# Windowed attention and ELU feed-forward on one core: the first chunk's probabilities kept in fp32 and turned on TensorE, and d_ff of the first two chunks in other parts

## The chip, the cores and the metric

The kernel runs on one core of a Trainium2 chip. The metric is the device time of one execution in microseconds. Before the change the median of three runs is 653.16 us (652.48 to 653.65).

## The reference

Causal attention with a window of 128 keys and 4 sink keys over 4 batches, 8 heads, 768 positions and a head size of 64, then a feed-forward over the 3072 tokens with 512 model columns, 2048 inner columns (d_ff) and ELU. The weights come in 64-bit floats, the rest in fp32.

```python
keep = is_sink | ((rel >= 0) & (rel < window))        # rel = query - key
scores = np.where(keep, q @ k.T / np.sqrt(D), -1e9)
a = np.exp(scores - scores.max(-1)); a = a / (a.sum(-1) + 1e-9)
x = (a @ v) laid out as [tokens, 512]
h = x @ w_in
out = np.where(h > 0, h, np.exp(np.minimum(h, 0)) - 1) @ w_out
```

## The kernel before

**Tiles.** Tokens are taken in 24 query tiles of 128, grouped into nine chunks (`SIZES`, L42: three of two tiles, six of three). Heads are taken in four pairs. A visit is one query tile of one head pair: its keys are its own tile and the one before it (the first tile of a batch has only its own), 132 columns each, the first 4 of them sinks.

**A visit (L572 to L683).** TensorE makes the scores of the two heads (L598 in the first chunks, fp32, one head on the upper and one on the lower 64 rows); VectorE adds the mask and takes the extremum (L617); ScalarE takes exp and the sum (L619); ScalarE or GpSimd scales the sum (L623) and VectorE inverts it (L624). Then the probabilities, times 1/sum, are split into two fp16 parts, high on ScalarE (L631) and low on VectorE (L632), into one tile `pq`. A DMA transpose from SyncE's queue (L650) turns `pq` into `pt`. V comes as a raw fp32 tile (`vs`, two buffers) and is split into fp16 high and low parts too (L545, L546). The values (L664) are three fp16 products for each head and key tile: high x high, low x high, high x low; later query tiles of a batch have sink values (L669) besides. The tiles of a chunk add up in one bank `po` for a head pair, from which x is taken in two fp16 parts (L701, L702).

**The feed-forward (L712 to L779).** For each of the 16 blocks f of d_ff: twelve products h of x and w_in (L729), ELU (exp on ScalarE, L737; L739 on VectorE or GpSimd; L740 on VectorE), split of g in two fp16 parts (L742, L743), and six products acc for a chunk of two tiles (nine for three) with w_out (L750). The weights stand in memory as 64-bit floats. Each half block is loaded (L434), rebuilt as fp32 by one ScalarE and three VectorE instructions (L305 to L308, through bank `acc[2]`), and split in fp16 parts by ScalarE (L455) and GpSimd (L456); its load waits for the high part of the half five before it. All halves then stay in SBUF.

**Order.** `PARTS` (L45) is the order of the feed-forward. Chunks 0 and 1 take turns over parts of d_ff. The sums of an unfinished part are stored to the output (L773) and added back later (L770, L771). Everything is a task with an engine, a duration and what it depends on; a planner (`Plan`, L99) places the tasks by a list schedule, TensorE's by positions in slots (two for each block and chunk), the others by due times from the round before, and `keep_order` holds each engine to that order. `RINGS` (L54) says how many buffers a tile has; a writer waits for the users of the buffer's last turn. Where a task has two possible engines, the planner chooses.

```python
PARTS = [(0, 0, HALF), (1, 0, HALF), (0, HALF, NF), (1, HALF, NF)] + ...   # HALF = 10, NF = 16
tr = add("SP", 1.4, lambda ...: nc.sync.dma_start_transpose(pt[:, :nblk, :], ...), deps=parts + ...)
val = add("PE", ..., values, deps=[tr, ...], pos=at[k - j + nt - 1] + V_AT0 + 0.01 * j, line=2)
```

Of the kernel before, what the change touches and what calls it, by code (L numbers as in the profile page):

```python
# [9 lines left out]
F32 = mybir.dt.float32  # L10
# [5 lines left out]
AF = mybir.ActivationFunctionType  # L16
ALU = mybir.AluOpType
# [3 lines left out]
P = 128  # L21
B, H, S, D = 4, 8, 768, 64
# [4 lines left out]
NF = FF // P  # L27
NW = 2 * NF
NS = 4
KW = NS + P  # L30
MASKED = -1.0e31

P_SCALE, V_SCALE = 16384.0, 2048.0
X_SCALE, W_SCALE = 32.0, 256.0
PO_SCALE = X_SCALE / (P_SCALE * V_SCALE)
# [5 lines left out]

SIZES = (2, 2, 2, 3, 3, 3, 3, 3, 3)  # L42

HALF = 10
PARTS = [(0, 0, HALF), (1, 0, HALF), (0, HALF, NF), (1, HALF, NF)] + [(c, 0, NF) for c in range(2, len(SIZES))]  # L45
LAG = 2
ROUNDS = 8
VISIT = 3
WHOLE = 4
DUP = 4  # L50
AHEAD = 5
V_AT = 7
V_AT0 = 5.0
RINGS = dict(kqs=2, kq=3, vs=2, vm=1, vt=6, sk=2, e=3, st=6, pq=3, pt=6, g=2, gh=3, x=7, wv=4, s=2, po=1, h=2, wu=2, sv=2, wps=1, raw=6)  # L54


def key_tiles(ch):
# [15 lines left out]
VT = NP * P  # L73
# [25 lines left out]
class Plan:  # L99
# [7 lines left out]
    def add(self, eng, dur, fn, *args, deps=(), lat=0.0, pos=None, or_=None, line=0, slow=1.0, lock=True):  # L107

        t = Task(eng, dur, fn, args, deps, lat, pos, slow)
        t.line = line  # L110
        t.lock = lock
        if or_:
            t.ways[or_[0]] = or_[1:]
        self.tasks.append(t)
        return t

    def ring(self, name, writers, users):

# [172 lines left out]
def dma_us(nbytes):  # L291
    return nbytes / 330e3
# [69 lines left out]
def fast_path(tc, ctx, first, kq, vx, wt, out, nw, flag):  # L362

    nc = tc.nc
    wide = wt.dtype != F32
    pool = ctx.enter_context(tc.tile_pool(name="sb", bufs=1))
    psum = ctx.enter_context(tc.tile_pool(name="ps", bufs=1, space=PSUM))

    def rows(name, shape, dtype, n=None, mem=pool):
        return [mem.tile(shape, dtype, name=f"{name}{i}") for i in range(n or RINGS[name])]  # L370

# [29 lines left out]
    tmp = pts[-1].rearrange("p b k -> p (b k)").bitcast(F32)  # L401
    rest = make_masks(nc, tmp[:, : 4 * P], tmp[:, 4 * P : 4 * P + NS], nw, m0, m1, m2)
    nc.gpsimd.memset(ones, 1.0)
    for t in pqs:
        nc.gpsimd.memset(t[:, 8, :], 0.0)

    plan = Plan()
    add, ring = plan.add, plan.ring
    turn = {}

    def slot(name):
        turn[name] = turn.get(name, -1) + 1
        return turn[name] % RINGS[name]

    rest_ = add("DVE", 0.9, rest)
# [11 lines left out]
    first_acc2 = []  # L427

    def weights(k):
# [10 lines left out]

        ld = add("SP", 0.4, load, deps=[w_done.get(k - AHEAD, [None])[0]], lat=1.45)
        if wide:
# [21 lines left out]
    base, pos = {}, 0  # L464
    for c, f0, f1 in PARTS:
        base.setdefault(c, pos)
        pos += 2 * (f1 - f0)


    xs = {}  # L470
    x_at, x_old = [0, 0], []

# [15 lines left out]
        x_old.append((lo, hi, users))  # L488

    later = []  # L490
    v_of, sk_of = {}, {}

    def attention(c):
        ts = CHUNKS[c]
        nt, kts = len(ts), key_tiles(ts)
        nk = len(kts)
        kc, qc = nk * KW, nt * P
        n = NP * nt
        if c == 0:
            at = [-3.0 - V_AT0 - 3.0 + 1.2 * (k - n) for k in range(n)]  # L500
        elif c == 1:
            at = [-1.0 + k * (base[c] - 1.0 - V_AT) / (n - 1) for k in range(n)]
        else:
            at = [base[c] - 2.0 - V_AT - (n - 1 - k) * (base[c] - base[c - 1]) / n for k in range(n)]

        def split_keys(h):
# [27 lines left out]
            lo = buf[:, KQ_MAX : KQ_MAX + kc] if c >= DUP else buf[:, kw : 2 * kw]  # L534
            return hi, lo, th, tl, users

        def vtile(g):

            if g not in v_of:
                st, i = vs[slot("vs")], slot("vt")  # L540
                ld = None
                if g not in first["vs_"]:
                    ld = add("SP", 0.4, lambda: nc.sync.dma_start(st, vx[:, g * VT : (g + 1) * VT]), lat=dma_us(P * VT * 4))
                hi, lo, users = vh[i], vl[i], []
                va = add("ACT", act_us(VT), lambda: nc.scalar.activation(hi, st, AF.Copy, scale=V_SCALE), deps=[ld])  # L545
                vb = add("DVE", 0.13 + 0.00108 * VT, lambda: nc.vector.scalar_tensor_tensor(lo, st, V_SCALE, hi, ALU.mult, ALU.subtract), deps=[va], slow=1.5)  # L546
                ring("vs", [ld or va], [va, vb])
                ring("vt", [va], users)
                v_of[g] = hi, lo, va, vb, users
            return v_of[g]  # L550
# [14 lines left out]
        k = 0  # L565
        for p in range(NP):
# [3 lines left out]
            po = po_ps[slot("po")]  # L570
            vals, visit = [], []
            for g in ts:  # L572
                t, j = g % NT, ts.index(g)
                nb = 1 if t == 0 else 2
# [5 lines left out]
                e3 = es[slot("e")]  # L580
                sm = sts[slot("st")]
                mn, rs, tmp = sm[:, 0:2], sm[:, 2:4], sm[:, 4 : 4 + 2 * NS].rearrange("p (e k) -> p e k", e=2)
                pq = pqs[slot("pq")]
                pt = pts[slot("pt")]
# [29 lines left out]
                exps, st_users = [], []  # L614
# [7 lines left out]

                rr = add("ACT", 0.22, lambda rs=rs: nc.scalar.activation(rs, rs, AF.Copy, scale=1.0 / P_SCALE, bias=1.0e-9 / P_SCALE), deps=[ex for _, ex in exps], or_=("POOL", 0.2, lambda rs=rs: nc.gpsimd.tensor_scalar(rs, rs, 1.0e-9, 1.0 / P_SCALE, ALU.add, ALU.mult)))  # L623
                rr = add("DVE", 0.17, lambda rs=rs: nc.vector.reciprocal(rs, rs), deps=[rr])  # L624
                parts, his = [], []
                for e in range(2):
                    src = e3[:, e, :wd].rearrange("p (b k) -> p b k", k=KW)[:, :, NS:]
# [4 lines left out]
                    b = add("DVE", 0.478 if nb == 2 else 0.33, lambda src=src, hi=hi, lo=lo, re=re: nc.vector.scalar_tensor_tensor(lo, src, re, hi, ALU.mult, ALU.subtract), deps=[a], slow=1.5)  # L632
                    parts += [a, b]
                    his.append(a)
                if t >= 2:
# [8 lines left out]
                    b = add("POOL", 0.65, sinks, deps=[rr], lock=False)  # L644
# [27 lines left out]
                if nt < VISIT:  # L672
                    val = add("PE", dur + 0.19 + (0.2 if j == 0 else 0.0), values, deps=[tr, *(d for v in vts for d in v[2:4]), *(sk[1:2] if sk else [])], pos=at[k - j + nt - 1] + (V_AT0 if c == 0 else V_AT) + 0.01 * j, line=2)
                    ring("pt", [tr], [val])
# [5 lines left out]
                else:  # L680
                    users = []
# [3 lines left out]
            if visit:  # L685
# [4 lines left out]

                val = add("PE", sum(v[1] for v in visit) + 0.19, together, deps=[*(v[2] for v in visit), *(d for v in visit for u in v[4] for d in u[2:4]), *(v[5][1] for v in visit if v[5])], pos=at[k - 1] + V_AT, line=2)
                for v in visit:
# [5 lines left out]
                vals.append(val)  # L698

            xh, xl = x_room(qc)  # L700
            fa = add("ACT", act_us(qc, True), lambda xh=xh, po=po: nc.scalar.activation(xh, po[:, :qc], AF.Copy, scale=PO_SCALE), deps=[vals[-1]])  # L701
            fb = add("DVE", dve_us(qc) + 0.1, lambda xh=xh, xl=xl, po=po: nc.vector.scalar_tensor_tensor(xl, po[:, :qc], PO_SCALE, xh, ALU.mult, ALU.subtract), deps=[fa])  # L702
            ring("po", [vals[0]], [fa, fb])
            users = []
            x_taken(fa, users)
            xs[c, p] = xh, xl, fa, fb, users


    evacs = [None] * max(SIZES)
    evacs[2] = first_acc2[-1] if first_acc2 else None  # L710

    def feed_forward(c, f0, f1, start):  # L712
        nt = len(CHUNKS[c])
# [68 lines left out]
    start = 0  # L782
    for c, f0, f1 in PARTS:
        if f0 == 0:
# [32 lines left out]
    b = add("PE", 0.1, lambda: nc.tensor.matmul(sp[:, 0:3], ones, some16, start=True, stop=True), deps=[a], pos=start + 2 * LAG - 1.5)  # L817
# [251 lines left out]
```

## Time and profile before

| | us |
|---|---|
| median of three runs | 653.16 |
| the profiled execution, as timed | 653.45 |
| its span, first to last instruction | 651.7 |
| TensorE busy in it | 615.2 |
| VectorE busy | 429.7 |
| ScalarE busy | 427.4 |
| GpSimd busy | 355.6 |

Durations come from the one profiled execution. PE is TensorE's matmuls, PEld its weight loads, DVE VectorE, ACT ScalarE, POOL GpSimd, SP SyncE; a q behind a name is the engine's sequencer. L598 is line 598 of the kernel. An fp32 product shows as two instructions, and "x4" counts instructions. In a timeline the number behind the start runs from the first one's start to the last one's end.

### The profile page before, as it was taken

Reading aid. Unit: us, or ns where it says so; the run is one execution under the profiler, and the core shown is the slowest. Engines: PE = TensorE matmul, PEld = TensorE weight load, DVE = VectorE, ACT = ScalarE, POOL = GpSimd, SP = SyncE. Lnnn points to the kernel's source line nnn. Section 1 sums busy time; section 2 is a strip of 40 time slices with the busy share of each in tenths; the row PEclk is TensorE's granted clock in tenths of the full one; section 3 lists DMA queues with packets and bytes.
Section 4 is the critical chain, followed back from the end, with each engine's and each line's share of the span. In section 5 each row is a group of like instructions: output and inputs, shape, how many; then the busy total and the mean of one; then the engine's idle time right before and its main releaser. Section 6 shows DMA issues by size and latency. Waiting matters only on the chain.

```text
span 651.7 us, 13258 instructions
## 1 busy us (share of the span) xinstructions
PE 615.2 (94%) x4449; PEld 364.5 (56%) x4449; DVE 429.7 (66%) x1175; ACT 427.4 (66%) x1227; POOL 355.6 (55%) x622
## 2 busy tenths in 40 slices
PE   3598789999999999999999999999999999999995
PEld 1354456666667556565555656565555656555552
DVE  6899988877756775557577766668577766433222
ACT  4797868767767876667667776667666775432221
POOL 1187879673436776655556766555456665313221
PEclk9997889999999999999999999999999999999998
DMA  7898887376637565346444755456655734201001
GB/s 281 166 258 264 278 186 227 122 193 139 162 90 147 141 158 123 78 110 187 120 100 108 225 113 135 85 114 167 131 101 103 202 83 101 65 34 39 1 0 54
DMA packets 124348, 87.84 MB, mean 135 GB/s; under 512 B 104176, under 2 KB 104176, under 8 KB 124272
## 3 DMA queue, kind: packets, MB, share of 16 engines
q1 hardware_dynamic: 124272, 86.92, 53.1%
q8 instruction: 37, 0.61, 0.4%
q14 instruction: 39, 0.32, 0.2%
HBM read 54.39 MB, written 7.34 MB: 95 GB/s over the span
## 4 chain that ended last, share of the span: by engine, by line
PE 86%; DVE 6%; DMA 3%; ACT 2%; issue 2%; POOL 1%; SPq 0%; DVEq 0%; ACTq 0%
PE h L729 38%; PE acc L750 37%; PE po L664 5%; PE s L598 2%; PE s L591 2%; PE s L592 2%; DMA pt<-pq 1%; DVE wu L307 1%; DVE wv L308 1%; DVE pq L632 1%; ACT e L619 1%; DVE wu L306 1%; DMA vs<-in_vx_dram 1%; DMA words<-in_window_dram 1%; DVE e L617 1%
## 5 line engine op out<-in xcount | busy, mean ns | idle before, releaser
L729 PE MATMUL h<-x,w 128*128 128x384 f16 (+1 forms) x1728 | 279.2, 312 | 2.2 <-ACT x L701 1.4
L729 PEld LDWEIGHTS <-w 128*128 128x128 f16 x1728 | 166.0, 99 | 99.5 <-issue 2.8
L743 POOL TENSOR_TENSOR gl<-g,gh 128x384 f16<-128x384 f32 (+1 forms) x144 | 126.4, 878 | 138.9 <-ACT gh L742 105.3
L750 PE MATMUL acc<-w,gh 128*128 128x512 f16 x768 | 194.1, 382 | 0.0
L737 ACT ACTIVATE g<-h 128x384 f32<-128x384 f32 (+1 forms) x144 | 65.5, 455 | 108.8 <-PE h L729 96.2
L632 DVE SCALAR_TENSOR_TENSOR pq<-e,st,pq 128x256 f16<-128x256 f32 (+1 forms) x192 | 110.0, 605 | 15.2 <-ACT pq L631 14.9
L750 PEld LDWEIGHTS <-gh 128*128 128x128 f16 x768 | 71.4, 98 | 71.5 <-ACT g L737 1.7
L750 PE MATMUL acc<-w,gl 128*128 128x512 f16 x384 | 109.6, 380 | 0.4 <-POOL gl L743 0.3
L739 DVE TENSOR_SCALAR g<-g 128x384 f32<-128x384 f32 (+1 forms) x76 | 36.9, 485 | 102.0 <-ACT g L737 101.9
L619 ACT ACTIVATE e<-e,st 128x264 f32<-128x264 f32 (+1 forms) x192 | 93.2, 486 | 15.3 <-DVE st L617 13.9
L617 DVE CUSTOM_DVE_ANT_0 e<-s,m 128x264 f32<-128x264 f32 (+1 forms) x192 | 71.5, 405 | 47.5 <-PE s L592 36.1
L631 ACT ACTIVATE pq<-e,st 128x256 f16<-128x256 f32 (+1 forms) x192 | 85.0, 480 | 14.6 <-DVE st L624 7.7
L742 ACT ACTIVATE gh<-g 128x384 f16<-128x384 f32 (+1 forms) x144 | 69.5, 483 | 35.1 <-DVE g L740 33.2
L740 DVE SCALAR_TENSOR_TENSOR g<-g,h 128x384 f32<-128x384 f32 (+1 forms) x144 | 72.7, 505 | 17.9 <-POOL g L739 16.3
L750 PEld LDWEIGHTS <-gl 128*128 128x128 f16 x384 | 37.6, 98 | 46.9 <-POOL gl L743 1.4
L526 POOL TENSOR_TENSOR kq<-kqs,kq 128x528 fp32r<-128x528 f32 (+1 forms) x40 | 49.3, 1232 | 22.6 <-ACT kq L522 22.4
L456 POOL TENSOR_TENSOR w<-wv,w 128x256 f16<-128x256 f32 x64 | 46.9, 752 | 13.4 <-ACT w L455 13.0
L598 PE MATMUL s<-kqs 64*128 64x264 f32 (+1 forms) x144 | 33.8, 498 | 19.3 <-DVE st L617 11.7
L739 POOL TENSOR_SCALAR g<-g 128x384 f32<-128x384 f32 (+1 forms) x68 | 33.8, 498 | 32.5 <-ACT g L737 30.1
L664 PE MATMUL po<-pt,vh 128*64 128x128 f16 x704 | 41.5, 228 | 7.1 <-DMA pt<-pq 5.5
L522 ACT ACTIVATE kq<-kqs 128x912 fp32r<-128x912 f32 (+1 forms) x40 | 36.3, 913 | 14.3 <-PE s L592 11.8
L528 POOL TENSOR_TENSOR kq<-kqs,kq 64x384 fp32r<-64x384 f32 x40 | 41.1, 1026 | 3.1
(81 smaller groups left out, 638.2 us busy)
## 6 DMA issues: line engine op xcount, KB each, us to landing
raw<-in_wt_dram SPq DMA_DIRECT2D x32, 512.0 KB, 5.2
kqs<-in_kq_dram SPq DMA_DIRECT2D x24, 456.0 KB, 3.7
kqs<-in_kq_dram SPq DMA_DIRECT2D x20, 390.0 KB, 3.6
vs<-in_vx_dram SPq DMA_DIRECT2D x28, 256.0 KB, 3.5
out_dram<-wv SPq DMA_DIRECT2D x24, 256.0 KB, 3.1
vm<-in_vx_dram SPq DMA_DIRECT2D x6, 768.0 KB, 4.8
kqs<-in_kq_dram SPq DMA_DIRECT2D x8, 326.0 KB, 4.0
pt<-pq SPq DMA_TRANSPOSE x96, 3.2
```

The lines of the kernel that those rows point to most:

```text
L617: red = add("DVE", 0.24 + 0.001 * wd, lambda ee=ee, me=me, sp=sps[e], m=m, wd=wd: nc.vector.tensor_tensor_reduce(ee, sp[:, :wd], m[:, :wd] ...
L619: ex = add("ACT", 0.47 + 0.00085 * wd, lambda ee=ee, me=me, rs=rs[:, e : e + 1]: nc.scalar.activation(ee, ee, AF.Exp, bias=me, scale=-1.0, ...
L631: a = add("ACT", act_us(nb * P, True), lambda src=src, hi=hi, re=re: nc.scalar.activation(hi, src, AF.Copy, scale=re), deps=[rr])
L632: b = add("DVE", 0.478 if nb == 2 else 0.33, lambda src=src, hi=hi, lo=lo, re=re: nc.vector.scalar_tensor_tensor(lo, src, re, hi, ALU.mult ...
L664: nc.tensor.matmul(po[e * D : (e + 1) * D, oc], vts[i][x][:, vo : vo + D], pt[:, (2 * e + part) * nb + i, :], start=new, stop=last)
L729: nc.tensor.matmul(hp[:, :n], win[:, part, d, :], xx[:, :n], start=k == 0, stop=k == 3 * ND - 1)
L737: a = add("ACT", act_us(n) + 0.18, lambda gf=gf, hp=hp, sums=sums: nc.scalar.activation(gf, hp[:, :n], AF.Exp, scale=1.0 / G_SCALE, accum_ ...
L739: b = add("DVE", 0.14 + 0.00057 * n, lambda gf=gf: nc.vector.tensor_scalar(gf, gf, -1.0, G_SCALE, ALU.add, ALU.mult), deps=[a], slow=2.1, ...
L740: b = add("DVE", dve_us(n), lambda gf=gf, hp=hp: nc.vector.scalar_tensor_tensor(gf, gf, 0.0, hp[:, :n], ALU.min, ALU.max), deps=[b])
L742: th = add("ACT", act_us(n), lambda gf=gf, gh=gh: nc.scalar.activation(gh[:, :n], gf, AF.Copy), deps=[b])
L743: tl = add("POOL", pool_us(n), lambda gl=gl, gf=gf, gh=gh: nc.gpsimd.tensor_tensor(gl[:, :n], gf, gh[:, :n], ALU.subtract), deps=[th])
L750: nc.tensor.matmul(acc[i], gg[:, i * P : (i + 1) * P], wout[:, part, :], start=f == f0 and k == 0, stop=f == f1 - 1 and k == 2)
```

## The change

For chunk 0 (`c < PLAIN`, with `PLAIN = 1`) the probabilities are not split and not transposed by DMA. GpSimd multiplies an identity by 1/sum into a diagonal matrix for each head; TensorE multiplies the exponentials as the stationary operand with it, which turns and scales them at once, in fp32, into `acc[0]` or `acc[1]`; ScalarE or VectorE copies the result to the `pt` buffer; and the values are one fp32 product for each head and key tile, with the raw V tile. V tile 0 is no longer split at all, and the raw tiles 0 and 1 stay in their buffers until chunk 0's last values. The parts of d_ff become 7 blocks of chunk 0, 13 of chunk 1, 9 of chunk 0 and 3 of chunk 1, in place of 10, 10, 6 and 6.

```diff
-HALF = 10
-PARTS = [(0, 0, HALF), (1, 0, HALF), (0, HALF, NF), (1, HALF, NF)] + [(c, 0, NF) for c in range(2, len(SIZES))]
+HALF = NF // 2
+PARTS = [(0,0,7),(1,0,13),(0,7,16),(1,13,16)] + [(c, 0, NF) for c in range(2, len(SIZES))]
+PLAIN = 1
+T_AT = 3.5
+PE_T, PE_V = 0.25, 0.25
+    ident = pool.tile([P, P], F32, name="ident")
+    make_identity(nc, ident)
...
+        def vraw(g):
+            if g not in raw_of:
+                st, users = vs[slot("vs")], []
...
+                ring("vs", [ld] if ld else [], users)
+                raw_of[g] = st, ld, users
+            return raw_of[g]
...
+                if c < PLAIN:
...
+                    def diagonal(dg=dg, rs=rs):
+                        nc.gpsimd.tensor_tensor(dg, ident.unsqueeze(1).to_broadcast([P, 2, P]), rs.unsqueeze(2).to_broadcast([P, 2, P]), ALU.mult)
+                    def turned(tp=tp, dg=dg, e3=e3, nb=nb):
+                        for e in range(2):
+                            for i in range(nb):
+                                o = (e * nb + i) * P
+                                nc.tensor.matmul(tp[:, o : o + P], e3[:, e, i * KW + NS : (i + 1) * KW], dg[:, e, :], start=True, stop=True)
+                    dgs = add("POOL", pool_us(2 * P), diagonal, deps=[rr])
+                    tr = add("PE", PE_T * 2 * nb, turned, deps=[dgs], pos=at[k] + T_AT, line=3)
+                    ev = add("ACT", act_us(2 * nb * P), ..., deps=[tr, rest_], or_=("DVE", dve_us(2 * nb * P), ...))
...
+                    def values(po=po, vts=vts, ptf=ptf, j=j, nb=nb, p=p):
...
+                                nc.tensor.matmul(po[e * D : (e + 1) * D, oc], vts[i][0][:, vo : vo + D], ptf[:, (e * nb + i) * P : (e * nb + i + 1) * P], start=j == 0 and i == 0, stop=j == nt - 1 and i == nb - 1)
+                    val = add("PE", PE_V * 2 * nb, values, deps=[ev, *(v[1] for v in vts)], pos=at[k - j + nt - 1] + V_AT0 + 0.01 * j, line=2)
```

## Rows read from the trace of the kernel before

**Rows 1.** The page: busy us, share of the span and instructions of each engine

```profile
PE 615.2 (94%) x4449; PEld 364.5 (56%) x4449; DVE 429.7 (66%) x1175; ACT 427.4 (66%) x1227; POOL 355.6 (55%) x622
```

**Rows 2.** Stretches: length, busy us (count) by engine, granted clock, DMA share, GB/s

```profile
0.00:37.38 37.38, 18.72 (x117) 11.40 (x118) 28.27 (x113) 25.61 (x74) 9.68 (x34) 1.00 0.79 217
37.38:90.80 53.42, 42.98 (x313) 25.23 (x314) 49.91 (x124) 42.99 (x122) 44.29 (x82) 0.90 0.93 269
90.80:159.00 68.20, 68.20 (x536) 43.63 (x536) 53.26 (x136) 51.39 (x157) 47.56 (x90) 0.97 0.62 168
```

**Rows 3.** TensorE's waits over the span: us in total, times, longest

```profile
PE s L598 <- DVE st L617: 11.7, 10, 2.8
...
PE po L664 <- DMA pt<-pq: 5.5, 5, 1.9
```

**Rows 4.** The chain that ended last, in order: start us, us, what

```profile
27.68 0.85 PE po L664 x12
...
37.38 2.61 PE h L729 x12
...
46.66 4.57 DMA vs<-in_vx_dram
...
90.80 2.50 PE h L729 x12
...
95.19 1.31 PE h L729 x12
96.50 1.29 PE acc L750 x6
...
105.61 0.46 PE po L664 x12
...
111.83 0.65 PE s L598 x4
```

**Rows 5.** VectorE, 37.38 to 90.8 us, by shape: count, busy us, mean ns

```profile
L306 DVE TENSOR_SCALAR wu<-raw 128x512 uint16<-128x512 uint16 x15 | 10.3, 683 | 0.0
L308 DVE SCALAR_TENSOR_TENSOR wv<-acc,wu 128x512 int32<-128x512 int32 x15 | 10.2, 680 | 0.4 <-ACT acc L305 0.3
L307 DVE TENSOR_SCALAR wu<-raw 128x512 uint16<-128x512 uint16 x15 | 10.1, 674 | 0.0
L632 DVE SCALAR_TENSOR_TENSOR pq<-e,st,pq 128x256 f16<-128x256 f32 x16 | 8.3, 553 | 0.0
L617 DVE CUSTOM_DVE_ANT_0 e<-s,m 128x264 f32<-128x264 f32 x17 | 6.6, 418 | 0.0
L740 DVE SCALAR_TENSOR_TENSOR g<-g,h 128x256 f32<-128x256 f32 x10 | 4.1, 411 | 2.3 <-POOL g L739 2.3
```

**Rows 6.** All engines from 0 to 37.38 us, by shape

```profile
L456 POOL TENSOR_TENSOR w<-wv,w 128x256 f16<-128x256 f32 x9 | 6.7, 772 | 7.4 <-ACT w L455 7.3
...
L632 DVE SCALAR_TENSOR_TENSOR pq<-e,st,pq 128x256 f16<-128x256 f32 x8 | 3.5, 479 | 0.0
...
L632 DVE SCALAR_TENSOR_TENSOR pq<-e,st,pq 128x128 f16<-128x128 f32 x8 | 2.4, 344 | 0.0
...
L702 DVE SCALAR_TENSOR_TENSOR x<-po,x 128x256 f16<-128x256 f32 x4 | 1.6, 406 | 0.0
...
L546 DVE SCALAR_TENSOR_TENSOR vl<-vs,vh 128x512 f16<-128x512 f32 x2 | 1.4, 680 | 0.0
```

**Rows 7.** TensorE in order of time: start us, us, instructions, idle before

```profile
6.38 0.81 PE L598 MATMUL s<-kqs 64*128 64x132 f32 x4 [6.38 <-DMA kqs<-in_kq_dram]
...
28.46 1.25 PE L598 MATMUL s<-kqs 64*128 64x264 f32 x4
...
45.06 0.71 PE L598 MATMUL s<-kqs 64*128 64x264 f32 x4
```

**Rows 8.** SyncE's queue in order of time, columns as in rows 7

```profile
26.78 7.17 SPq L650 DMA_TRANSPOSE pt<-pq  x3
```

**Rows 9.** Instructions on raw weights to 130 us: ns min/median/max, first and last start

```profile
L306 DVE TENSOR_SCALAR wu<-raw x31: 433/545/949, 12.8 to 124.9; 128x512 uint16<-128x512 uint16 x31
```

More of the change, by code (lines that the diff above doesn't have):

```diff
@@ L51 @@
 AHEAD = 5
+PLAIN = 1
 V_AT = 7
 V_AT0 = 5.0
-RINGS = dict(kqs=2, kq=3, vs=2, vm=1, vt=6, sk=2, e=3, st=6, pq=3, pt=6, g=2, gh=3, x=7, wv=4, s=2, po=1, h=2, wu=2, sv=2, wps=1, raw=6)
+T_AT = 3.5
+PE_T, PE_V = 0.25, 0.25
+RINGS = dict(tp=2, tp_=2, kqs=2, kq=3, vs=2, vm=1, vt=6, sk=2, e=3, st=6, pq=3, pt=6, g=2, gh=3, x=7, wv=4, s=2, po=1, h=2, wu=2, sv=2, wps=1, raw=6)
 def key_tiles(ch):
@@ L467, in fast_path @@
         pos += 2 * (f1 - f0)
+    evacs = [None] * max(SIZES)
+    evacs[2] = first_acc2[-1] if first_acc2 else None
     xs = {}
@@ L490, in fast_path @@
     later = []
-    v_of, sk_of = {}, {}
+    raw_of, v_of, sk_of = {}, {}, {}
     def attention(c):
@@ L535, in split_keys @@
             return hi, lo, th, tl, users
-        def vtile(g):
-            if g not in v_of:
-                st, i = vs[slot("vs")], slot("vt")
+        def vraw(g):
+            if g not in raw_of:
+                st, users = vs[slot("vs")], []
                 ld = None
@@ L543, in vtile @@
                     ld = add("SP", 0.4, lambda: nc.sync.dma_start(st, vx[:, g * VT : (g + 1) * VT]), lat=dma_us(P * VT * 4))
+                ring("vs", [ld] if ld else [], users)
+                raw_of[g] = st, ld, users
+            return raw_of[g]
+        def vtile(g):
+            if g not in v_of:
+                st, ld, raw_users = vraw(g)
+                i = slot("vt")
                 hi, lo, users = vh[i], vl[i], []
@@ L546, in vtile @@
                 vb = add("DVE", 0.13 + 0.00108 * VT, lambda: nc.vector.scalar_tensor_tensor(lo, st, V_SCALE, hi, ALU.mult, ALU.subtract), deps=[va], slow=1.5)
-                ring("vs", [ld or va], [va, vb])
+                raw_users += [va, vb]
                 ring("vt", [va], users)
@@ L624, in attention @@
                 rr = add("DVE", 0.17, lambda rs=rs: nc.vector.reciprocal(rs, rs), deps=[rr])
+                if c < PLAIN:
+                    dg = pq[:, :4, :].rearrange("p b k -> p (b k)").bitcast(F32).rearrange("p (e k) -> p e k", e=2)
+                    tp = acc[slot("tp")]
+                    ptf = pt.rearrange("p b k -> p (b k)").bitcast(F32)[:, : 2 * nb * P]
+                    def diagonal(dg=dg, rs=rs):
[7 more added lines that the diff above has]
+                    tr = add("PE", PE_T * 2 * nb, turned, deps=[dgs], pos=at[k] + T_AT, line=3)
+                    ev = add("ACT", act_us(2 * nb * P), lambda ptf=ptf, tp=tp, n=2 * nb * P: nc.scalar.activation(ptf, tp[:, :n], AF.Copy), deps=[tr, rest_], or_=("DVE", dve_us(2 * nb * P), lambda ptf=ptf, tp=tp, n=2 * nb * P: nc.vector.tensor_scalar(ptf, tp[:, :n], 1.0, None, ALU.mult)))
+                    ring("e", [r for r, _ in exps], [tr])
+                    ring("st", [r for r, _ in exps], [dgs])
+                    ring("pq", [dgs], [tr])
+                    ring("tp", [tr], [ev])
+                    evacs[slot("tp_")] = ev
+                    vts = [vraw(g - nb + 1 + i) for i in range(nb)]
+                    def values(po=po, vts=vts, ptf=ptf, j=j, nb=nb, p=p):
+                        oc = slice(j * P, (j + 1) * P)
+                        for i in range(nb):
+                            for e in range(2):
+                                vo = p * P + e * D
+                                nc.tensor.matmul(po[e * D : (e + 1) * D, oc], vts[i][0][:, vo : vo + D], ptf[:, (e * nb + i) * P : (e * nb + i + 1) * P], start=j == 0 and i == 0, stop=j == nt - 1 and i == nb - 1)
+                    val = add("PE", PE_V * 2 * nb, values, deps=[ev, *(v[1] for v in vts)], pos=at[k - j + nt - 1] + V_AT0 + 0.01 * j, line=2)
+                    ring("pt", [ev], [val])
+                    vals.append(val)
+                    for v in vts:
+                        v[2].append(val)
+                    k += 1
+                    continue
@@ L700, in attention @@
             xh, xl = x_room(qc)
-            fa = add("ACT", act_us(qc, True), lambda xh=xh, po=po: nc.scalar.activation(xh, po[:, :qc], AF.Copy, scale=PO_SCALE), deps=[vals[-1]])
-            fb = add("DVE", dve_us(qc) + 0.1, lambda xh=xh, xl=xl, po=po: nc.vector.scalar_tensor_tensor(xl, po[:, :qc], PO_SCALE, xh, ALU.mult, ALU.subtract), deps=[fa])
+            to_x = X_SCALE / P_SCALE if c < PLAIN else PO_SCALE
+            fa = add("ACT", act_us(qc, True), lambda xh=xh, po=po, to_x=to_x: nc.scalar.activation(xh, po[:, :qc], AF.Copy, scale=to_x), deps=[vals[-1]])
+            fb = add("DVE", dve_us(qc) + 0.1, lambda xh=xh, xl=xl, po=po, to_x=to_x: nc.vector.scalar_tensor_tensor(xl, po[:, :qc], to_x, xh, ALU.mult, ALU.subtract), deps=[fa])
             ring("po", [vals[0]], [fa, fb])
@@ L706, in attention @@
             xs[c, p] = xh, xl, fa, fb, users
-    evacs = [None] * max(SIZES)
-    evacs[2] = first_acc2[-1] if first_acc2 else None
     def feed_forward(c, f0, f1, start):
```

## The prediction

> **What bounds the kernel now.** I read the busy shares first, then the stretches, then TensorE's waits, then the chain that ended last. TensorE is busy for 94% of the span and none of the other engines for more than 66% [rows 1], so the kernel as a whole is a TensorE kernel, and only a stretch in which TensorE is not the bound can give anything back. The stretches show where that is [rows 2]. From 90.8 us on TensorE has no gap: 68.20 of 68.20 us to 159 us, and none of its waits lies behind that point; the largest kinds, scores on VectorE's reductions and values on the transposes, are 11.7 and 5.5 us in the whole span [rows 3]. Before 90.8 us it is busy for 18.7 of 37.4 us and 43.0 of 53.4 us. In the middle stretch VectorE is the engine that is full: 49.91 of 53.42 us, a share of 0.934, while ScalarE has 43.0 and GpSimd 44.3.
>
> The chain says the same [rows 4]. It goes through TensorE alone from there on. At 90.80 us the feed-forward of chunk 1 begins: chunk 0's first ten d_ff blocks lie ahead of it, from 37.38 us. Dense, a block costs 1.31 us for its twelve products h and 1.29 us for its six products acc, together 2.60 us; ten of them should take 26.0 us, and chunk 1's attention, eight visits of 0.65 us of scores and 0.46 us of values, 8.9 us more. They took 53.4 us. So about 18.5 us are lost there, partly as gaps, partly as clock: the twelve h of 37.38 us took 2.61 us, 217 ns for 256 columns, which is the 1.2 GHz level, those of 95.19 us 1.31 us, which is the 2.4 GHz level. (The granted clock in rows 2 is 1.00 for the first stretch although the durations there are those of the lower level; I go by durations.) What VectorE does in the middle stretch is mostly weights [rows 5]: L306, L307 and L308 each ran 15 times, 30.6 of its busy time, 2.04 us for each half block of weights. By 90.8 us 20 halves had to be ready, ten blocks of two.
>
> I count the order of the feed-forward in slots, two per block, 1.30 us each. Chunk 1 starts at slot 20 before and at slot 14 after; chunk 2 starts at slot 64 in both, and behind that nothing differs.
>
> **The change, part by part.** *The parts.* With 7, 13, 9, 3 blocks only 14 halves of weights, not 20, are needed before chunk 1 starts; blocks 7 to 12 are needed from slot 28 to 38 (before: 7 to 9 by slot 18, 10 to 12 from slot 40), and 13 to 15 from slot 52. Chunk 1's attention is needed six slots earlier. Had everything behind it been dense, starting chunk 1 at slot 14 is worth as much as before's state at 90.8 - 6 x 1.30 = 83.0 us. So the gain is 83.0 us less the time T at which slot 14 is reached, less what is lost between slot 14 and slot 64.
>
> *VectorE's work before T.* Before, it was busy for 28.27 + 49.91 = 78.2 us up to 90.8 us [rows 2]. Gone: six halves of weights, 6 x 2.04 = 12.2 us; chunk 0's low halves of the probabilities, eight of 479 ns and eight of 344 ns [rows 6], 5.9 us (their 2.4 and 3.5 us busy time); the low half of V tile 0 (tile 0 is no key of chunk 1), 0.7 us at 680 ns [rows 6]; three g of 411 ns [rows 5], 1.2 us. Together 20.0 us. Added: eight copies of the turned probabilities from PSUM, four of 256 columns and four of 512, which may go to ScalarE or to VectorE. No such copy is in the trace. The nearest rows are L702 at 406 ns for 256 columns [rows 6] and L308 at 680 ns for 512 [rows 5]: 4 x (0.41 + 0.68) = 4.4 us if all go to VectorE, nothing if all go to ScalarE; I take half, 2.2 us, since both engines are about equally full there. That leaves 60.4 us. ScalarE, with 68.6 us busy up to there [rows 2], loses sixteen high halves, six halves of weights and three g, and gets at most eight copies; it is not the bound.
>
> From work to time there are two bounds. With the idle time that VectorE had before (90.8 - 78.2 = 12.6 us), T is 73.0 us; with the share that it had (0.861), 70.2 us. TensorE itself could be there by about 60 us (chunk 0's x at 32.5, 7 x 2.60 + 8.9 behind it). I take 72 us: the idle time ahead of the first scores, which wait for their load until 6.38 us [rows 7], doesn't shrink. Gain so far 11 us.
>
> *Chunk 0's attention.* Per visit the two high halves on ScalarE, the two low ones on VectorE and the DMA transpose go. The transposes are what the values waited for last, five times, 5.5 us in all [rows 3], and they hold SP's queue, the waits between them counted, as the three that take 7.17 us from 26.78 us on [rows 8]. New: on GpSimd a product of the doubled identity with 1/sum (256 columns; the nearest row is L456, 772 ns [rows 6]; GpSimd is busy for 9.7 of 37.4 us), on TensorE 2 or 4 fp32 products of 128 columns, the copy (0.41 or 0.68 us), and 2 or 4 fp32 products with raw V in place of 6 or 12 in fp16. Over the eight visits that is 24 + 24 fp32 products. Nothing in the trace is an fp32 product over all 128 rows. The scores are fp32 products over 64 rows, two of them side by side: 1.25 us at the lower level for the pair with 264 columns when it follows other work, 0.71 us at the higher [rows 7], so for 128 columns 0.61 and 0.34 us. The low bound is half of the latter, 0.17 us, if a full-height product costs what one of a pair costs; the high bound is the 0.81 us that a lone pair of 132 columns took at the lower level [rows 7]. I take 0.61 us for a turn and 0.45 for a value product (two heads write different halves of the partitions) at the lower level, 25.4 us in all, half of it at the higher. The fp16 values that they replace cost 0.85 us for a visit of twelve [rows 4], half for six, 5.1 us in all.
>
> So TensorE's list for chunk 0 from 10.0 us on is 7.4 us of scores (4 x (0.81 + 1.25) - 0.81 [rows 7]) and 25.4 us, 32.8 us at the lower level. In the trace the level rose at about 40 us, behind the first stretch in which TensorE had no gaps (the lower level at 37.38 us [rows 4], the higher at 45.06 [rows 7]); this list leaves few, so I take 10 us of it at the lower level and the rest at the higher: 10 + 10 + 22.8/2 = 31.4 us, with the copies behind it about 32, and the first x product at about 32.5 instead of 37.4 us. This matters as the time from which VectorE gets blocks to feed, and stands in T already; the product sizes matter only if they carry x beyond 45 us (below).
>
> The Trainium skill (FP8 and Floating Point Precision, TensorE Precision Notes) says that true FP32 takes 4 passes through the array. By that a 128-column product would cost 4 x 128 / 1.2 GHz = 0.43 us at the lower level, an estimate, in place of my 0.61 and 0.45: chunk 0's x a few us earlier, T unchanged. The 0.71 us of the pair at the higher level [rows 7] lies between 0.44 (its two products fully side by side) and 0.88 us.
>
> *V and the queue.* The raw V tiles 0 and 1 stay in both staging buffers until chunk 0's last values, so the loads of V tile 2 and of the sinks, which waited only for tile 0's split before, move to about 31 us. A V load takes about 4.6 us to land [rows 4], and chunk 1's values come behind several blocks of the feed-forward. Hidden, and one landing, 4.6 us, if not. The loads stand in SP's queue, and weight loads behind them; SP loses eight transposes, so its queue gets shorter. The identity on GpSimd falls into its idle time before 10 us.
>
> *Slots 14 to 40.* Here VectorE has 12 halves of weights (24.5 us), 13 g (5.3 us), about three visits of chunk 2, which is spread from slot 11 on (3 x (0.84 + 1.11) = 5.9 us [rows 5], with 0.3 us each for the small instructions 6.8), and a V tile and an x (1.1 us): 37.7 us, at the share 0.934 40.4 us. TensorE needs 13 x 2.60 + 3 x 1.11 = 37.1 us. So 3 us of it is lost as waits for weights. From slot 40 to 64 VectorE has three blocks left and 12 g, and fits.
>
> **Sum.** 653.45 us profiled (its span 651.7) - 11 + 3 = 645.5 us; the median of the runs lies 0.29 us below the profiled one, so 645.2 us.
>
> Against the change speaks that VectorE's shifts are not of one length: single ones of L306 run from 433 to 949 ns [rows 9], and they average 683 ns in the middle stretch [rows 5], where GpSimd is busy for 44.3 of 53.4 us [rows 2]. The change puts eight GpSimd products into the first stretch; if each lengthens one shift by the difference of the ends, 0.52 us, that is 4 us of VectorE at most, nothing at least, and I take T's 72 us to hold it. The Trainium skill (SBUF — State Buffer, Who interferes with whom) says VectorE and GpSimd share a port pair and the second one blocks fully; by that the upper end, 4 us less gain, would hold (649 us); the longest shift, 949 ns, agrees with such a block.
>
> **Rivals.** *A, the start doesn't move or the weights come late* (24%): VectorE does chunk 2's visits ahead of the weights between slots 14 and 40 (five more visits, 11 us of VectorE, of which TensorE hides 5.9 us), or the work saved before T is not usable because the loads of weights wait for earlier halves. Gain 11 - 3 - 6 = 2 us: 651 us. For it: chunk 2's scores are placed there; against it: the planner orders by due time, and weights are due earlier.
> *B, the whole slack comes back* (14%): VectorE idle for the 6.4 us until the first scores and little more, T = 60.4 + 7.6 = 68 us, no waits in slots 28 to 40: gain 15 us, 638.5 us. For it: 15 us of idle VectorE in 90.8 to 159 us [rows 2].
> *C, slower* (12%): the fp32 products become chunk 0's bound. At 0.81 us each, never side by side and never at the higher level, 48 cost 38.9 us, with the scores 46.3 from 10 us on: x at 56.3 us, T = 56.3 + 18.2 + 8.9 = 83.4 us, 0.4 us later than 83.0; with the 3 us of slots 14 to 40 as in the forecast 3.4 us are lost: 657 us. It decides where T passes 80 us, so from x at 53 us, 0.74 us per product. Against it: the row at 1.25 us [rows 7]; for it: TensorE stays at the lower level until 40 us in this trace, whatever its fp32 work.
>
> **How the numbers follow.** The forecast has 50% (its own range 641 to 650 us), A 24%, B 14%, C 12%. 0.2% (1.3 us) is what can be told from no change. Faster: the forecast, B and half of A (its 651 us lies just beyond that bound), 0.77; the rest of A is the same, 0.11; slower is C, 0.12. The range goes from B's middle, 638, to where A ends, 653.
>
> **What would show it.** Right: no transposes before 35 us; the first h products at 30 to 35 us; chunk 1's feed-forward (the eighth group of twelve h) at 70 to 74 us; VectorE over 0.9 full from 32 us to then; waits of h for weights of 2 to 4 us between 90 and 112 us; L729 with 384 columns first at 206 instead of 214 us. Wrong: x of chunk 0 later than 45 us, or TensorE's waits continuing beyond 115 us, or gaps before 70 us as long as now.

## The result, and the profile after

The changed kernel takes 643.69 us (642.79 to 644.91), the one before 653.19 us (652.48 to 653.65): a ratio of 0.9871, with a 95% interval of 0.9851 to 0.9890. The forecast was 645.2 us in 638 to 653. The profiled execution took 644.91 us, its span 643.1 us, 8.6 us shorter than before's 651.7.

The busy line of the page, to be held against [rows 1]:

```profile
PE 614.6 (96%) x4473; PEld 367.4 (57%) x4473; DVE 424.7 (66%) x1165; ACT 421.4 (66%) x1214; POOL 359.0 (56%) x629
```

TensorE is busy for as long as before, though it now has the fp32 products: the time came out of its idle time (span less busy), 651.7 - 615.2 = 36.5 us before, 643.1 - 614.6 = 28.5 us after. The stretches, columns as in [rows 2]; slot 14, where the feed-forward of chunk 1 begins, is at 75.70 us, and slot 40 at about 114.5:

```profile
0.00:36.53 36.53, 24.15 (x141) 16.49 (x141) 24.26 (x100) 19.41 (x60) 13.83 (x41) 0.91 0.56 194
36.53:75.70 39.17, 29.87 (x256) 18.17 (x255) 34.77 (x93) 32.83 (x94) 29.94 (x63) 0.91 0.83 231
75.70:114.50 38.80, 38.32 (x304) 24.94 (x303) 37.23 (x90) 33.49 (x96) 33.41 (x58) 1.00 0.76 248
```

VectorE's work up to slot 14 is 24.26 + 34.77 = 59.0 us (the sum said 60.4), but it is only 0.89 full between 36.53 and 75.70 us, where the forecast had over 0.9. From slot 14 on TensorE lacks 0.48 us in 38.80. Its waits over the span, all ahead of 78 us:

```profile
PE s L614 <- DVE st L633: 6.7, 4, 3.0
PE s L614 <- DMA kqs<-in_kq_dram: 6.6, 1, 6.6
PE po L718 <- DVE x L757: 3.3, 1, 3.3
PE acc L653 <- POOL pq L647: 1.8, 2, 1.5
PE h L782 <- DVE g L793: 1.7, 2, 1.4
```

Against [rows 3] the scores' waits for VectorE fell from 11.7 to 6.7 us, and the values' waits for transposes are gone (in two kernels below that have the fp32 attention too, e4 and e6, those of later chunks cost 2.6 and 2.4 us). New are 1.8 us for GpSimd's diagonals and a single 3.3 us for the po bank. TensorE in order of time, as in [rows 7], chunk 0 first:

```profile
13.75 1.23 PE L653 MATMUL acc<-pq,e 128*128 128x128 f32 x4 [0.33 <-POOL pq L647]
16.09 2.07 PE L653 MATMUL acc<-pq,e 128*128 128x128 f32 x8
...
21.10 1.16 PE L653 MATMUL acc<-pq,e 128*128 128x128 f32 x8
23.32 0.66 PE L670 MATMUL po<-pt,vs 128*64 128x128 f32 x8 [0.32 <-DVE pt L657]
26.01 1.23 PE L653 MATMUL acc<-pq,e 128*128 128x128 f32 x4 [1.49 <-POOL pq L647]
...
30.35 0.70 PE L670 MATMUL po<-pt,vs 128*64 128x128 f32 x4
...
36.53 1.48 PE L782 MATMUL h<-x,w 128*128 128x256 f16 x12
...
50.31 2.63 PE L782 MATMUL h<-x,w 128*128 128x256 f16 x12
...
59.99 0.43 PE L718 MATMUL po<-pt,vh 128*64 128x128 f16 x4 [3.30 <-DVE x L757]
...
75.70 1.38 PE L782 MATMUL h<-x,w 128*128 128x256 f16 x11
...
206.23 1.96 PE L782 MATMUL h<-x,w 128*128 128x384 f16 x11
```

Each fp32 product is two instructions. Eight of them, four turns, take 2.07 us at 16.09 and 1.16 us at 21.10: the two clock levels, 0.52 and 0.29 us a turn. The first twelve h start at 36.53 us, 0.78 us sooner than before (37.31 in this view; the chain of [rows 4] has 37.38). Slot 14 comes at 75.70, and the first product of 384 columns at 206.23 us (213.78 before): 7.55 of the 8.6 us are won by then.

What holds the middle stretch is in the chain that ended last, as in [rows 4], around the longest of the new waits:

```profile
48.78 0.25 DVE e L633
49.03 5.81 DMA vs<-in_vx_dram
54.84 0.02 issue
54.87 0.64 ACT vh L561
...
56.14 0.68 DVE wv L311
56.82 0.60 DVE wu L309
57.42 0.81 DVE wu L310
...
58.94 0.67 DVE wv L311
59.61 0.34 DVE x L757
59.95 0.04 issue
59.99 0.85 PE po L718 x12
```

The load of V tile 3 starts at 49.03 us and lands 5.81 us later; the last values of a chunk 1 pair wait for its split, and the eviction of that pair's x then stands on VectorE behind instructions on weights (L309 to L311). The po bank is free only after it. This late tile is not new: before, its load started at 46.66 us and stood on the chain too [rows 4].

### The profile page after: what moved, and what is told of

It is laid out like the page before. It is cut to its first block, busy times and chain, and to the rows that moved or that the text cites. A ratio compares the mean times of both kernels' runs of the same rounds, so it can differ in the third digit from the quotient of the medians.

```text
span 643.1 us, 13253 instructions
## 1 busy us (share of the span) xinstructions
PE 614.6 (96%) x4473; PEld 367.4 (57%) x4473; DVE 424.7 (66%) x1165; ACT 421.4 (66%) x1214; POOL 359.0 (56%) x629
## 4 chain that ended last, share of the span: by engine, by line
PE 90%; DMA 2%; DVE 2%; POOL 2%; issue 2%; ACT 1%; SPq 0%; DVEq 0%; POOLq 0%; ACTq 0%
PE h L782 38%; PE acc L803 38%; PE po L718 5%; PE s L614 3%; PE s L607 2%; PE s L608 2%; PE acc L653 1%; DMA vs<-in_vx_dram 1%; POOL w L461 1%; DMA words<-in_window_dram 1%; DMA kqs<-in_kq_dram 1%; PE po L723 1%; POOL gl L796 0%; PE po L670 0%; DVE e L633 0%
## 5 line engine op out<-in xcount | busy, mean ns | idle before, releaser
L686 DVE SCALAR_TENSOR_TENSOR pq<-e,st,pq 128x256 f16<-128x256 f32 (+1 forms) x176 | 103.0, 618 | 14.2 <-ACT pq L685 14.1
L633 DVE CUSTOM_DVE_ANT_0 e<-s,m 128x264 f32<-128x264 f32 (+1 forms) x192 | 71.7, 405 | 46.4 <-PE s L608 36.6
L685 ACT ACTIVATE pq<-e,st 128x256 f16<-128x256 f32 (+1 forms) x176 | 78.3, 483 | 12.3 <-DVE st L640 6.5
L614 PE MATMUL s<-kqs 64*128 64x264 f32 (+1 forms) x144 | 29.0, 457 | 13.3 <-DVE st L633 6.7
L607 PE MATMUL s<-kq 128*128 128x264 f32 (+1 forms) x120 | 41.3, 365 | 0.0
```

The lines of the kernel that those rows point to most:

```text
L607: nc.tensor.matmul(sp[:, :wd], q, hi[:, c0 : c0 + wd], start=True, stop=False)
L633: red = add("DVE", 0.24 + 0.001 * wd, lambda ee=ee, me=me, sp=sps[e], m=m, wd=wd: nc.vector.tensor_tensor_reduce(ee, sp[:, :wd], m[:, :wd] ...
L685: a = add("ACT", act_us(nb * P, True), lambda src=src, hi=hi, re=re: nc.scalar.activation(hi, src, AF.Copy, scale=re), deps=[rr])
```

## The experiments

My theory in the expectations is V: VectorE's work sets T, the time of the slot at which chunk 1's feed-forward begins. Results by kernel, in us. The median and the ratio to the kernel before, with its interval, are over all runs; the other columns come from the one profiled execution: its span, the first h of chunk 0, T with its slot, the time from slot 14 to the end (T moved to slot 14 with 1.30 us a slot, then taken from the span), and TensorE's idle time. The row "before" has its times from the chain in [rows 4].

| kernel | median | ratio | span | first h | T (slot) | slot 14 to end | idle |
|---|---|---|---|---|---|---|---|
| before | 653.19 | 1 | 651.7 | 37.38 | 90.80 (20) | 568.7 | 36.5 |
| after | 643.69 | 0.9871 [0.9851, 0.9890] | 643.1 | 36.53 | 75.70 (14) | 567.4 | 28.5 |
| e9_after_again | 642.60 | 0.9847 [0.9822, 0.9871] | 640.8 | 33.62 | 73.04 (14) | 567.8 | 26.9 |
| e1_parts_only | 648.87 | 0.9945 [0.9930, 0.9959] | 645.9 | 39.22 | 76.95 (14) | 569.0 | 34.9 |
| e2_plain_only | 647.39 | 0.9910 [0.9892, 0.9928] | 646.9 | 36.30 | 86.66 (20) | 568.0 | 29.0 |
| e3_one_shift_less | 639.54 | 0.9798 [0.9784, 0.9813] | 639.6 | 34.10 | 73.20 (14) | 566.4 | 25.8 |
| e5_diag_on_act | 646.94 | 0.9930 [0.9913, 0.9948] | 643.5 | 33.71 | 74.09 (14) | 569.4 | 29.7 |
| e4_parts_5_11 | 642.68 | 0.9861 [0.9841, 0.9882] | 640.9 | 36.58 | 65.42 (10) | 570.3 | 27.4 |
| e8_parts_9_14 | 642.92 | 0.9852 [0.9831, 0.9873] | 643.3 | 35.63 | 81.02 (18) | 567.5 | 29.3 |
| e6_three_v_buffers | 641.09 | 0.9832 [0.9809, 0.9854] | 639.3 | 33.70 | 69.53 (14) | 569.8 | 28.7 |
| e10_v3_ahead6 | 643.46 | 0.9864 [0.9843, 0.9884] | 640.5 | 35.85 | 71.39 (14) | 569.1 | 28.5 |
| e11_v3_one_shift_less | 639.22 | 0.9801 [0.9779, 0.9824] | 635.0 | 34.60 | 68.04 (14) | 567.0 | 26.3 |
| e12_before_v3 | 647.24 | 0.9906 [0.9885, 0.9928] | 646.2 | 36.86 | 87.01 (20) | 567.0 | 33.8 |
| e13_parts_v3 | 653.73 | 1.0041 [1.0027, 1.0055] | 651.9 | 42.56 | 83.37 (14) | 568.5 | 39.7 |

Read within one execution, the end follows T. From slot 14 to the end all fourteen executions take 566.4 to 570.3 us, while slot 14 itself moves by 15 us and the span by 17 us. A median is another matter: the profiled run may lie at either end of the runs it is taken from. e3 and e11 have nearly the same median, 639.54 and 639.22 us, and profiled runs of 641.39 and 636.78 us. So T is held against the span here, and kernels are compared by their ratios.

**The two halves of the change.** The kernel before with the new parts alone:

```diff
-PARTS = [(0, 0, HALF), (1, 0, HALF), (0, HALF, NF), (1, HALF, NF)] + ...
+PARTS = [(0,0,7),(1,0,13),(0,7,16),(1,13,16)] + ...
```

> The kernel before with the parts 7, 13, 9, 3 and nothing else. Theory V (VectorE's work ahead of chunk 1's feed-forward sets the time T at which that begins, and behind it TensorE is dense): VectorE loses six halves of weights and three g, 13.4 us, ahead of slot 14, so T is about 77 us against 75.7 in the changed kernel, and the time is 645 to 648 us. Rival S (the gain is chunk 0's fp32 attention, the parts only move waits): no more than 1 us below the kernel before, 652 to 653 us.

and the changed kernel with the old parts, so that only chunk 0's fp32 attention is new:

```diff
-PARTS = [(0,0,7),(1,0,13),(0,7,16),(1,13,16)] + ...
+PARTS = [(0,0,10),(1,0,10),(0,10,16),(1,10,16)] + ...
```

> The changed kernel with the parts of before, 10, 10, 6, 6: only chunk 0's attention is in fp32. Theory V: VectorE loses 4 to 6 us of work ahead of slot 20, which comes at 85 to 87 us instead of 90.8; time 648 to 650 us. Rival S: nearly the whole gain, 644 to 646 us. If the two parts need each other, this one is at 652 to 653 us.

Both win, 0.55% and 0.90%; multiplied, 0.9945 x 0.9910 = 0.9855, within the interval of the whole change. Neither is the other's cover, so S is out. V had both T right (76.95 and 86.66 us); the times lie 0.9 us above and 0.6 us below its ranges. By idle time the fp32 attention does what it was expected to (36.5 to 29.0 us); the parts alone leave it nearly as it was (34.9), and most of their gain is busy time, 615.2 to 611.0 us for the same 4449 products: the first h of chunk 1, which took 2.56 us in the kernel before in this view, are at the higher clock level. e1 also shows weights late, which the forecast had for slots 14 to 40; TensorE in order of time:

```profile
76.95 1.49 PE L729 MATMUL h<-x,w 128*128 128x256 f16 x12
...
114.67 1.38 PE L729 MATMUL h<-x,w 128*128 128x256 f16 x11 [1.53 <-POOL w L456]
```

In the changed kernel that wait is gone.

**Less work for VectorE.** In the changed kernel one of three shifts for every half of weights is left out (L310 there; the sign of the weights is not computed):

```diff
-            u2 = add("DVE", 0.446, step(2), deps=[ld], slow=2.0)
+            u2 = None
```

> The changed kernel without the VectorE instruction that takes the sign of each weight (the second shift of each half block, 0.68 us; all weights come out positive). Theory V: 14 of them lie ahead of slot 14, 9.5 us of VectorE, so T falls from 75.7 to 67 to 70 us and the time to 635 to 639 us. Rival: T is set by TensorE's own chain (products of chunk 0, clock, chunk 1's attention): T stays within 2 us and the time at 642 to 644 us.

The median fell by 4.2 us, 3.1 below the changed kernel's second set, and the ratio's interval meets neither of theirs. T is 73.20 us, in a run of 641.39 us; the changed kernel itself had 75.70 and 73.04. V's 67 to 70 us is missed, and the time lies between V's range and the rival's. The edit is a weaker test than its fourteen instructions of 0.68 us (9.5 us) suggest, because the planner filled the gap: it brought the scores of two more visits forward and gave VectorE one more copy of turned probabilities and three tasks of L794 (the g step L739 of before), which have two possible engines. VectorE's work up to T is 25.11 + 31.17 = 56.3 us, only 2.8 us less than in the changed kernel's first profile. What can be read is the stretch from first h to T; e3's two stretches, then those of e9, the changed kernel with no edit:

```profile
0.00:34.10 34.10, 22.80 (x141) 15.40 (x142) 25.11 (x100) 20.51 (x62) 16.44 (x48) 1.00 0.64 222
34.10:73.20 39.10, 31.84 (x265) 18.58 (x264) 31.17 (x93) 30.59 (x90) 26.11 (x57) 0.91 0.88 241
```

```profile
0.00:33.62 33.62, 21.51 (x140) 14.84 (x141) 23.32 (x100) 19.40 (x60) 13.93 (x41) 1.00 0.61 210
33.62:73.04 39.42, 31.80 (x256) 19.15 (x255) 34.76 (x93) 32.81 (x94) 29.92 (x63) 0.83 0.80 229
```

VectorE has 3.6 us less to do there and is 0.80 full, and the stretch is as long as before, 39.10 beside 39.42 us (39.17 in the first profile): in this order VectorE's work is not what limits that stretch. Its chain goes through a load of weights (5.23 us at 46.46) and GpSimd instead. The two visits done ahead of T, 1.3 us of scores, agree with e3 being the quickest of all from slot 14 to the end.

**The diagonal on another engine.**

```diff
-                        nc.gpsimd.tensor_tensor(dg, ident..., rs..., ALU.mult)
+                        for e in range(2):
+                            nc.scalar.activation(dg[:, e, :], ident, AF.Copy, scale=rs[:, e : e + 1])
-                    dgs = add("POOL", pool_us(2 * P), diagonal, deps=[rr])
+                    dgs = add("ACT", 2 * act_us(P, True), diagonal, deps=[rr])
```

> The changed kernel with the diagonal matrices made on ScalarE (two copies of 128 columns with a scale, about 0.34 us each) instead of GpSimd, where one product stood behind weight splits and TensorE waited 1.5 us for it. Theory V: chunk 0's x comes 1 to 2 us earlier, but T hangs on VectorE and the end stays within 1 us, 643 to 645 us. Rival: the chain through chunk 0's products sets T: the whole of 1.5 to 2 us shows at the end, 641.5 to 642.5 us. If ScalarE is short of time, up to 2 us slower, 646 us.

The first h came at 33.71 us and T at 74.09, but the kernel is slower than the changed one, beyond all three expectations: the intervals (0.9913 to 0.9948 and 0.9851 to 0.9890) do not meet. A copy took 0.39 us on ScalarE. Behind T TensorE has gaps that it doesn't have in the changed kernel:

```profile
74.10:112.00 37.90, 35.48 (x283) 23.03 (x281) 34.27 (x73) 31.44 (x87) 31.90 (x54) 1.00 0.74 232
```

2.4 us are missing here, 0.48 there; 1.5 of them are a wait for GpSimd's split of weights. In this order GpSimd was the better place for the diagonal.

**Where slot 14 lies.** The changed kernel again, with no edit, and with two other divisions of the blocks:

> The changed kernel as it is, beside the others of this set. All theories: 643 to 645 us, its ratio to the kernel before 0.985 to 0.989 as in the result.

```diff
+PARTS = [(0,0,5),(1,0,11),(0,5,16),(1,11,16)] + ...    (e4)
+PARTS = [(0,0,9),(1,0,14),(0,9,16),(1,14,16)] + ...    (e8)
```

> The changed kernel with parts of 5, 11, 11 and 5 blocks. Theory V (VectorE's halves of weights set T): each block fewer ahead of chunk 1 takes 4.5 us of VectorE off T and gives 2.6 us of TensorE's work back, so two blocks fewer gain 3 to 4 us if the later weights still come in time: 640 to 642 us, and slot 10 at 66 to 68 us. Rival W (chunk 1's attention, not weights, is then what T waits for, or the weights of block 5 on, needed from slot 20, come late): T at 70 us or later or waits for weights behind it, 644 to 648 us.

> The changed kernel with parts of 9, 14, 7 and 2 blocks. Theory V: two blocks more ahead of chunk 1, 9 us more of VectorE against 5.2 us of TensorE's work: 3 to 4 us slower than the changed kernel, 647 to 648 us, close to the kernel with only chunk 0 in fp32. Rival W: T is not set by weights but by chunk 1's attention, so it loses nothing: 643 to 645 us.

V's sum (VectorE's work as the prediction counts it, plus the 12.6 us of before) predicted T well here, 64 and 82 us against 65.42 and 81.02, and 77.4 and 86.4 for e1 and e2 against 76.95 and 86.66. But neither division changes the time: 642.68 and 642.92 us beside 642.60, where V had 640 to 642 and 647 to 648. With slots of 1.30 us, e4 has slot 14 at 65.42 + 4 x 1.30 = 70.6 us, 5.1 us ahead of the changed kernel's first profile and 2.4 us ahead of its second, with a span 2.2 us shorter than the first and as long as the second; e8 has it at 75.8 us, with the span of the first. So e4 gives 2.5 to 2.9 us back behind slot 14. TensorE from slot 14 to the end, in the changed kernel and in e4:

```profile
75.70:643.10 567.40, 560.61 (x4081) 332.71 (x4079) 365.65 (x974) 369.19 (x1062) 315.18 (x526) 1.00 0.49 124
```

```profile
70.64:640.90 570.26, 561.60 (x4076) 332.39 (x4074) 369.68 (x970) 370.16 (x1064) 317.02 (x525) 1.00 0.49 123
```

It is not work left for later: e4 has no more products there than the changed kernel, 4076 and 4081. It has 8.7 us of gaps instead of 6.8, and its products take 1.0 us longer. So 7 and 13 is one of several divisions with the same time.

**A third staging buffer for V**, against the wait in the chain above: in the changed kernel, the same with a longer look-ahead, with the shift left out as in e3, and in the kernel before.

```diff
-RINGS = dict(... vs=2, ...)
+RINGS = dict(... vs=3, ...)     (e6, e10, e11, e12, e13)
-AHEAD = 5
+AHEAD = 6                       (e10)
```

> The changed kernel with three buffers for raw V tiles in place of two. In the changed kernel the load of V tile 3 starts at 49.0 us and lands at 54.8, and TensorE then waits 0.9 us for its split and 3.3 us for the x behind it. Theory V: VectorE is full in that stretch whatever comes when, so T moves by less than 1 us and the time stays at 643 to 645 us. Rival B (the late V tile itself costs): those 3 to 4 us go, T at 72 us, 640 to 641 us.

> The changed kernel with three raw V buffers and with each load of weights waiting for the half six before it, not five. If loads of weights hold VectorE up ahead of chunk 1's feed-forward, T falls by 2 us or more below the 69.5 us of the kernel with three V buffers and the time to 638 to 640 us. If VectorE has its weights in time anyway, no difference to three V buffers alone, 640 to 642 us.

> Three raw V buffers and, as in the earlier experiment, no VectorE instruction for the sign of the weights (left out). With two V buffers that shift less moved T by 2.5 us where its 14 instructions have 9.5 us. Theory V2 (VectorE was the bound, and without the shift the late V tile and the loads took its place): with three buffers T falls from 69.5 us by 4 to 9 us, 61 to 65 us, and the time to 634 to 637 us. Rival (TensorE's own chain of chunk 1's attention and of blocks is what is left): T stays at 67 to 70 us, time 637 to 640 us.

> The kernel before with three raw V buffers only. There V tile 3 is loaded at 46.7 us too. If the third buffer is worth something by itself, 650 to 651 us; if only the changed kernel holds raw tiles long enough to need it, 652 to 653 us as before.

In e6 the staging is off the chain: V tile 3 is loaded at 33.23 us (SyncE's queue), 15.8 us sooner than after, and T falls to 69.53 us, further than rival B had it (72).

```profile
33.23 0.38 SPq L550 DMA_DIRECT2D vs<-in_vx_dram  x1
```

From first h to T:

```profile
33.70:69.53 35.83, 28.42 (x255) 17.05 (x255) 35.49 (x94) 32.47 (x93) 30.09 (x60) 0.95 0.97 252
```

VectorE is 0.99 full, with as much work up to T as after (59.5 us), and most of the chain up to 60 us runs through it. In e11, with 4.6 us less work for it up to T, T falls by 1.5 us more only, and VectorE is 0.88 full (29.45 of 33.44 us). What stands behind it then is loads of weights; e11's chain, in order:

```profile
45.04 5.91 DMA raw<-in_wt_dram
...
56.43 4.01 DMA raw<-in_wt_dram
...
64.84 4.22 DMA raw<-in_wt_dram
```

T there is as the rival to V2 had it, though not by TensorE's own chain. The longer look-ahead gives nothing where VectorE has all its work (e10, 643.46 us, intervals that overlap with e6's); with the shift left out, where the loads hold, it was not tried.

e6 takes 1.5 us less than the changed kernel beside it (e9), with overlapping intervals: not shown by the medians. Its slot 14 is 3.5 us ahead of e9's and its span 1.5 us shorter. It too gives back 2.0 us in gaps and not in work: 4081 products behind slot 14 in both, busy for 560.6 us in both, and two waits for transposes between 69.6 and 160 us are 1.5 us of the gaps. e11 has slot 14 5.2 us ahead of e3 and a span 4.6 us shorter, though the medians are nearly the same. In the kernel before, the same buffer is worth 0.94%, as much as the fp32 attention and more than was expected; T comes 3.7 us earlier.

**The same buffer with the parts alone**, the last run:

> The kernel before with the parts 7, 13, 9, 3 and three raw V buffers, so the changed kernel with three V buffers less its fp32 attention of chunk 0. Theory V (the fp32 attention takes 4 to 5 us of work off VectorE, whatever the buffers): 645 to 646.5 us, ratio to the kernel before 0.988 to 0.990, 4 to 5 us above the 641.1 us of the changed kernel with three V buffers. Rival B (what the fp32 attention was worth is what a late V tile or a full staging buffer cost, so that a third buffer gives the same): 641 to 642.5 us, ratio 0.982 to 0.985.

Both theories miss. It is the only kernel that is slower than before, and 1% slower than e1, from which it differs by that buffer. The first h comes at 42.56 us, and two transposes stand on its chain:

```profile
24.77 6.38 DMA pt<-pq
...
33.72 5.04 DMA pt<-pq
```

TensorE's waits in it:

```profile
PE po L664 <- DMA pt<-pq: 9.9, 6, 2.8
```

That is 5.5 us before [rows 3], and nothing after. A buffer added to a planned order re-plans all of it; here two of chunk 0's transposes landed late, and why these did was not tested. The fp32 attention, which has no transposes in chunk 0, is never that late: its first h lies at 33.6 to 36.6 us in all nine kernels that have it, and at 36.9 to 42.6 in the four without. So what it is worth depends on the order: 0.9% alone (e2), 0.7% beside the new parts (after against e1), 2.1% beside parts and buffer (e6 against e13).

## Why the prediction was right, step by step

- **TensorE's gaps ahead of chunk 1's feed-forward are what is to be had**: right. Idle time fell by 8.0 of the 8.6 us, and ahead of T alone from 29.1 to 21.7 us.
- **VectorE's work up to slot 14**: 60.4 us forecast, 59.0 measured. The copies of the turned probabilities split as taken: five of eight on VectorE, 2.7 us (2.2 taken). The shifts that GpSimd's products might have lengthened took 583 and 634 ns on average (L309 and L310 up to T), less than the 683 and 674 ns of [rows 5].
- **T at 72 us**: the step that was off. 75.70 us in the first profile, 73.04 in the second; 73.0 was the upper bound. The forecast has 32.5 us to the first h and 39.5 from there to T; measured were 36.53 + 39.17 and 33.62 + 39.42. So the second term held, and all of the delay is chunk 0's. There the forecast had no wait for GpSimd's diagonals, and it measured 1.8 us in both executions; the rest of the first execution's delay is mostly clock (last section). VectorE's idle time ahead of T, taken as 12.6 us, was 75.70 - 59.0 = 16.7 us, and 15.0 in the second.
- **The move of V's loads**, costed at nothing or one landing: nothing. Tile 2 and the sinks moved to 35.63 and 36.05 us (31 forecast), and nothing waited for them. The tile that TensorE waits for is number 3, whose load moved by +2.4 and -0.6 us only; it was late before as well, and a third buffer gains as much of T there (3.7 us) as in the changed kernel (3.5 against e9).
- **3 us lost in slots 14 to 40**: wrong. Slot 40 came 38.80 us after slot 14, with 0.48 us of gaps, although VectorE was 0.96 full there. A wait for weights of 1.5 us appears in e1, not in the changed kernel.
- **A term left out**: before, the first block of chunk 1 ran at the lower clock level, twelve h in 2.50 us against 1.31 [rows 4] and six acc in 1.89 us against 1.29, 1.8 us in all. After, T's eleven h take 1.38 us. So the sum should read: slot 14 in a dense before at 83.0 + 1.8 = 84.8 us, less 75.7, a gain of 9.1 us; the spans differ by 8.6. The acc stand in the chain before, behind the h of 90.80 us:

```profile
93.30 1.89 PE acc L750 x6
```

- **The number**: in part luck. T was 3.7 us late, and the 3 us of loss and the 1.8 us of clock, 4.8 together, went the other way.
- **Chunk 0's prices**: a first turn pair took 1.23 us at the lower level, 0.61 each as taken, in a longer run 0.52, at the higher 0.29; value products 0.35 and 0.17 us (0.45 and half of it taken). Four passes, as the Trainium skill has it (FP8 and Floating Point Precision, TensorE Precision Notes), would be 0.43 us for a turn at the lower level, an estimate; the measured 0.52 decides.
- **No transposes early, first 384-column product**: the first transpose in SyncE's queue is at 38.73 us (after 35, as forecast), the product at 206.23 us (206).
- **Rival A** (the start doesn't move): out, T is 75.7 or less; **B** (T at 68, 638.5 us): not with the change as it is; with the third buffer and a shift less T is 68.04 us, in an execution of 636.78 us; **C** (fp32 products bound): out, x came at 36 us, not 53, and e2, which has the fp32 attention alone, is faster.

What remains open: why kernels with an earlier slot 14, e4 and e6 above all, have 2 us more of gaps behind it; and why VectorE's idle time ahead of T differs by up to 7 us with the order.

## What to carry to other kernels

Where one engine is full from some point on, the gain is the time at which that point is reached: here the end followed it within 4 us over fourteen executions. The point can be summed from the feeding engine's work, but the idle time on top of it belongs to the order of the work, not to the engine, and it lay between 10.0 us (e6) and 16.9 us (e3). Hold a time read in a trace against the end of that same execution; held against the medians alone, T looks in e4 and e11 as if it were worth nothing. Where a planner fills what an edit frees, count what the engine then does before the edit is called a test of that engine. Test one such change in more than one order: the same buffer was worth 0.94% in one kernel here and cost 1% in another.

## What the runs showed of the hardware

The two profiled executions of the changed kernel start differently. In the second (e9) the turn after the wait of 1.5 us for GpSimd ran at the higher clock level, not the lower one as in the first; TensorE in order of time:

```profile
25.64 0.71 PE L653 MATMUL acc<-pq,e 128*128 128x128 f32 x4 [1.50 <-POOL pq L647]
26.28 0.72 PE L614 MATMUL s<-kqs 64*128 64x264 f32 x4
26.93 1.16 PE L653 MATMUL acc<-pq,e 128*128 128x128 f32 x8
```

The same products took 1.23 us for the pair and 2.07 us for the four in the first profile. Up to that wait the two were 0.4 us apart; first h came 2.9 us later in the first, T 2.7 us and the end 2.3 us. So one profile against one cannot place T to better than some 3 us, which is as much as T moved in e3. Why the level fell in the one and not in the other is not shown: the gap ahead is 1.49 and 1.50 us.
